# Two units earlier: the casts and copies of V in a fused window attention and MLP

## Chip, cores and metric

One core of a Trainium2 chip. The metric is the time on the device in microseconds (us) of one execution of the whole kernel; inputs and output lie in the chip's memory (HBM), and each time is a median over several runs.

The engines are named as the profile names them: PE is TensorE (matmuls; PEld its weight loads), ACT is ScalarE, DVE is VectorE, POOL is GpSimd, SP is SyncE, which here does nothing but issue DMAs. Each engine works through its own queue of instructions in the order in which the program was written, and waits where an instruction needs something that is not there.

## The reference

Causal attention within a window of 64 positions (8 batches, 8 heads, 576 positions, 64 per head), then a layer norm, an MLP with ReLU and a residual:

```python
def _attn_ref(q, k, v):
    scores = scale * np.matmul(q, k.transpose(0, 1, 3, 2))
    rel = pos[:, None] - pos[None, :]
    mask = (rel >= 0) & (rel < window)
    scores = np.where(mask, scores, -1000000000.0)
    ...
    attn = attn / (np.sum(attn, axis=-1, keepdims=True) + 1e-09)
    return np.matmul(attn, v).astype(np.float32)

def _moe_ref(x, g_ln, w_ch1, w_ch2):
    xn = (x - mu) / np.sqrt(var + 1e-06) * g_ln
    ch = np.maximum(xn @ w_ch1, 0.0) @ w_ch2
    return (x + ch).astype(np.float32)
```

`x` has 576 positions of 512 features in each batch; the hidden layer has 2048.

## The kernel before

**Blocks and stages.** The work is cut into nine groups of 512 positions. Groups 0 to 7 ("blocks") are the first 512 positions of each batch; group 8 collects the last 64 positions of all eight batches, in four "tails" of two batches each. The program runs one stage per group: stage `g` is the MLP of group `g`. The attention of the next block, `g+1`, is written in between, and so are the loads and the casts to fp16 of the block after it, `g+2`.

**Units and slots.** `mlp_units(g)` gives a list of small pieces of PE work. From stage 2 on they are 16 units `l1(hc)` (four matmuls of 128x512 each and one ReLU on ACT that writes `hrT`), then 14 units `product(n, t)` (eight matmuls of 128x256 each; some end in an addition on DVE, `post`). The loop at the end of the function writes unit `i`, then everything that was put in slot `i` with `at(i, f, ...)`, in the order in which it was put there. This alone sets the order of each engine's queue: nothing is moved afterwards. An instruction that is put at a later unit simply stands later in its engine's queue.

**One block's attention.** `s_mm(b, j)` (L326) makes the scores of a quarter of a block on PE, ACT takes the exponential into `pt` (`s_exp`, L347), DVE masks it (`s_mask`, L367), and `b_step(b, j)` (L383) multiplies by V. `b_step` then has DVE divide, take mean and variance (`mv`), and `r_step` has ACT make the reciprocal standard deviation from `mv` in two small instructions (L403, L404). `z_step` normalises on DVE (L414), and for quarters 0 to 2 a transposing DMA from SP (`x_step`, L461), for quarter 3 PE and ACT (`zt_step`, L450 and L453), turn it into `zT`, the MLP's input.

**V in two positions.** A window of 64 queries needs its own 64 keys and the 64 before them. `b_step` therefore reads V from two tiles: `vA`, the fp16 cast of the block's V, and `vB`, the same shifted by half a group of partitions. From block 3 on (`b >= NPE`) positions are interleaved in pairs, and `make_vB` copies `vA` to `vB` by four DMAs from POOL: for each half `j` (0 and 64) a copy of a whole run of 32 partitions, all four chunks `c` (L205, 130 KB), and a copy of the other 32 partitions for the first three chunks, shifted by one chunk (L206, 97.5 KB). `b_step(b, 0)` reads chunk 0 of `vB`, which the L206 copies don't write. `keep_v` (L132) then copies the last positions of V for the tails, two small DMAs more. All three are put in slots of stage `b - 2`; `b_step(b, 0)` stands at unit 4 of stage `b - 1`.

**The step around the change.** In stages 2 to 5 the casts for block `n = g + 2` all stand in the products of the stage, and on ACT: four of q and k (`cast_q`, L143, 128x1024), whose results SP transposes by DMA (`x_main`, L279 and L283), and four of V (`cast_v`, L143, 128x512, one for each chunk `c`). Between them ACT has `r_step` of the last quarter of block `g+1` (from `steps`, slot 19) and its `zt_step` copy (slot 23). Block 3 is prepared in stage 1, with its casts on POOL, but by the same `make_vB`. SP's queue goes from `x_main` straight on to the loads of q, k and V for the next block, and POOL's from `keep_v` to the stores of the stage's output (L469).

**The tails.** The table `TAILS[6]` puts the preparation of group 8 into stage 6: `load_tail`, `cast_tail` (part 0 is q and k, parts 1 and 2 are V into the tile `vt8`; the last argument says whether ACT or POOL casts), `x_tail` (the transposing DMA, L292), `x_prev` (a copy of the keys before the tail, on ACT for tails 1 to 3, L300), and the first scores. A row with `b_step` in slot `u` also puts its `r_step` in slot `u + 1` and its `z_step` in slot `u + 2`.

**PSUM buffers.** The results of `l1` and of the products share a pool of two buffers (`mm`) and another of two (`tp`); a matmul that starts a new result waits until the buffer that it was given has been read by ACT or DVE.

Of the kernel before, what the change touches and what calls it, by code (L numbers as in the profile page):

```python
# [18 lines left out]
def kernel(  # L19
# [182 lines left out]
    def make_vB(b):  # L202
        if b >= NPE:
            for j in range(0, 128, 64):
                nc.gpsimd.dma_start(out=vB[b][j + 32:j + 64, :], in_=vA[b][j:j + 32, :])  # L205
                nc.gpsimd.dma_start(out=vB[b][j:j + 32, 1:4], in_=vA[b][j + 32:j + 64, 0:3])  # L206
            return
        nc.gpsimd.dma_start(out=vB[b][64:128, :], in_=vA[b][0:64, :])
        nc.gpsimd.dma_start(out=vB[b][0:64, 1:4], in_=vA[b][64:128, 0:3])
# [231 lines left out]
    def pace(t):  # L441
        nc.gpsimd.tensor_copy(out=tok, in_=t)
# [302 lines left out]
    def tail_casts(i, act, *us):  # L745
        return tuple((u, cast_tail, i, part, act) for part, u in enumerate(us))
# [3 lines left out]
            *tail_casts(0, False, 7, 9, 9), (8, x_tail, 0), (8, x_prev, 0), (8, load_tail, 2, 0), (8, load_tail, 2, 1),  # L750
            *tail_casts(1, False, 10, 12, 12), (11, x_tail, 1), (12, load_tail, 3, 0), (12, load_tail, 3, 1),
            (18, x_prev, 1), (17, s_mm, 8, 0), (21, s_mask, 8, 0), *tail_casts(2, True, 19, 20, 20), (19, x_tail, 2), (20, x_prev, 2),
            *tail_casts(3, True, 22, 25, 25), (23, x_tail, 3), (25, x_prev, 3), (24, b_step, 8, 0),
            (24, s_mm, 8, 1), (26, s_mask, 8, 1)),
        7: ((1, b_step, 8, 1), (1, s_mm, 8, 2), (3, s_mask, 8, 2), (3, zt_step, 8, 0),
            (6, b_step, 8, 2), (6, s_mm, 8, 3), (8, s_mask, 8, 3), (7, zt_step, 8, 1),
# [2 lines left out]
    for g in range(NGRP):  # L759
# [3 lines left out]
        def at(i, f, *a):  # L763
            slots[min(i, len(slots) - 1)].append((f, a))
# [72 lines left out]
        if g == 1:  # L837
# [19 lines left out]
            for c in range(4):  # L857
                at(5 + c, cast_v, 2, c, c + 1)
            at(8, make_vB, 2)
            at(9, keep_k, 1)  # L860
            at(9, keep_v, 1)
# [38 lines left out]
        if 0 < g and b + 1 < B:  # L900
            n = b + 1
            e = 3 if g == 1 else 1
            at(e, load_qk, n, 0)
            at(e + 1, load_qk, n, 1)
            at(e + 4, load_v, n, 0, 4)
            if g == 1:
                at(10, alloc_qkT, n)
                for j, (x, half) in enumerate(((0, 0), (1, 0), (0, 1), (1, 1))):
                    u = (16, 19, 22, 25)[j]
                    at(u, lambda j=j: pace(rcps[(b, j)][:, 0:1]))  # L910
                    at(u, cast_q, n, x, half)
                at(20, x_main, n, 0)
                at(26, x_main, n, 1)
                at(19, alloc_v, n)
                at(19, alloc_vB, n)
                for u, c, j in ((21, 0, 0), (22, 1, 0), (25, 2, 1), (27, 3, 2)):
                    at(u, (lambda j=j: pace(zT[b][:, 0, 128 * j:128 * j + 1])) if c % 2 == 0 else
                       (lambda j=j: pace(rss[(b, j)])))
                    at(u, cast_v, n, c, c + 1)
                at(27, make_vB, n)  # L920
                at(27, keep_v, n)
            else:
                at(6, keep_k, b)
                at(3, alloc_qkT, n)
                for u, x, half in ((16, 0, 0), (16, 1, 0), (17, 0, 1), (19, 1, 1)):
                    at(u, cast_q, n, x, half, True)
                at(18, x_main, n, 0)
                at(21, x_main, n, 1)
                at(18, alloc_v, n)
                at(18, alloc_vB, n)  # L930
                for c in range(4):
                    at(21 + c, cast_v, n, c, c + 1, True)
                at(25, make_vB, n)
                at(25, keep_v, n)
        for i, u in enumerate(units):
            cur[0] += 1
            u()
# [34 lines left out]
```

## Time and profile before

| | us |
|---|---|
| median of 13 runs | 313.02 (310.42 to 317.29) |
| the profiled execution | 313.63 |
| its span, first to last instruction | 311.7 |
| PE busy in the span | 289.3 |
| ACT busy | 190.7 |
| DVE busy | 192.6 |
| POOL busy | 104.0 |

How to read the rows of a profile. In a timeline a row is: start in us from the span's start, duration, engine, line of the kernel, operation, tile written `<-` tiles read, shapes, and how many like instructions were merged; in square brackets, where the engine was idle before it, for how long and what ended the wait. The durations of neighbours on one engine overlap a little, because an engine starts on the next instruction before the last one has left it. A row of the waits is: who waited `<-` for whom: us in total, times, the longest. A DMA's row on an engine is only the time that the issue takes; how long the data take until they have landed is shown apart.

The page divides the span in 40 slices; PE's clock is granted in full in all but the last, and the mean granted clock is 0.996.

### The profile page before, as it was taken

Reading aid. Unit: us, or ns where it says so; the run is one execution under the profiler, and the core shown is the slowest. Engines: PE = TensorE matmul, PEld = TensorE weight load, DVE = VectorE, ACT = ScalarE, POOL = GpSimd, SP = SyncE. Lnnn points to the kernel's source line nnn. Section 1 sums busy time; section 2 is a strip of 40 time slices with the busy share of each in tenths; the row PEclk is TensorE's granted clock in tenths of the full one; section 3 lists DMA queues with packets and bytes.
Section 4 is the critical chain, followed back from the end, with each engine's and each line's share of the span. In section 5 each row is a group of like instructions: output and inputs, shape, how many; then the busy total and the mean of one; then the engine's idle time right before and its main releaser. Section 6 shows DMA issues by size and latency. Waiting matters only on the chain.

```text
span 311.7 us, 7942 instructions
## 1 busy us (share of the span) xinstructions
PE 289.3 (93%) x3259; PEld 186.8 (60%) x3259; DVE 192.6 (62%) x353; ACT 190.7 (61%) x372; POOL 104.0 (33%) x193
## 2 busy tenths in 40 slices
PE   5678999999998999799989996999999999999993
PEld 2446544865844578347845783479557844784582
DVE  0676337367854896289638952897389866742361
ACT  1688743676935875587558744885685967406500
POOL 3669765996674004300340043002363010000000
PEclk9999999999999999999999999999999999999998
DMA  7999999999959989997998999859998940003005
GB/s 178 257 381 331 316 279 291 270 304 260 201 85 296 214 100 201 287 212 93 219 284 207 99 215 281 199 77 187 264 146 155 158 152 2 2 0 135 2 0 135
DMA packets 115379, 58.23 MB, mean 187 GB/s; under 512 B 82048, under 2 KB 108160, under 8 KB 115344
## 3 DMA queue, kind: packets, MB, share of 16 engines
q1 hardware_dynamic: 110672, 45.50, 68.8%
q0 software_dynamic: 3712, 11.72, 11.9%
q10 hardware_dynamic: 960, 0.53, 0.6%
q8 instruction: 25, 0.41, 0.6%
q14 instruction: 10, 0.08, 0.1%
HBM read 36.70 MB, written 9.44 MB: 148 GB/s over the span
## 4 chain that ended last, share of the span: by engine, by line
PE 67%; DMA 15%; DVE 4%; SPq 4%; POOL 3%; ACT 3%; issue 2%; ACTq 0%; POOLq 0%; DVEq 0%
PE hps L509 27%; PE wX L587 12%; DMA vB<-vA 11%; PE wZ L587 6%; PE hph L546 5%; PE wY L587 4%; PE xps L383 4%; PE ch L560 3%; DMA w1s<-in_moe_w_ch_dram 2%; SPq L171 2%; PE sc L326 2%; DMA qk<-in_k_dram 2%; SPq L81 1%; ACT vA L143 1%; PE ztp L450 1%
## 5 line engine op out<-in xcount | busy, mean ns | idle before, releaser
L509 PE MATMUL hps<-zT,w1g 128*128 128x512 f16 x480 | 109.9, 379 | 0.7 <-ACT hrT L513 0.7
L513 ACT ACTIVATE hrT<-hps 128x512 f16<-128x512 f32 x120 | 71.3, 596 | 50.4 <-PE hps L509 49.2
L509 PEld LDWEIGHTS <-w1g 128*128 128x128 f16 x480 | 44.9, 98 | 50.4 <-issue 1.0
L587 PEld LDWEIGHTS <-sw 128*128 128x128 f16 x448 | 43.5, 98 | 5.0
L205 POOL DMA_DIRECT2D vB<-vA x10 | 5.1, 510 | 98.5 <-ACT vA L143 98.2
L587 PEld LDWEIGHTS <-hrT 128*128 128x128 f16 x336 | 32.4, 98 | 5.4
L367 DVE TENSOR_TENSOR pt<-pt,mask 128x1024 f16<-128x1024 f16 x28 | 20.8, 743 | 20.3 <-ACT pt L347 12.6
L347 ACT ACTIVATE pt<-sc 128x512 f16<-128x512 f32 x40 | 23.7, 594 | 9.1 <-PE sc L326 9.1
L469 POOL DMA_DIRECT2D out_dram<-osb x20 | 13.1, 658 | 47.6 <-DVE osb L605 43.5
L392 DVE BATCH_NORM_STATS2 stats<-xn 128x6 f32<-128x512 f32 x36 | 25.0, 694 | 1.2
L390 DVE TENSOR_TENSOR xn<-xps,rcp 128x512 f32<-128x512 f32 x36 | 24.9, 691 | 1.2
L546 PE MATMUL hph<-zT,w1g 128*128 128x256 f16 x192 | 23.7, 273 | 1.6 <-POOL w1g L235 1.6
L498 DVE TENSOR_TENSOR sw<-hrT 128x1024 f16<-128x1024 f16 x28 | 19.0, 677 | 9.7 <-ACT hrT L513 9.7
L383 PEld LDWEIGHTS <-pt 128*64 128x64 f16 x576 | 12.2, 110 | 20.4 <-issue 15.4
L414 DVE TENSOR_SCALAR z<-xn,mv,rs 128x512 f16<-128x512 f32 x32 | 17.8, 557 | 10.3 <-ACT rs L404 10.1
L387 DVE RECIPROCAL rcp<-xps 128x8 f32<-128x8 f32 x36 | 7.4, 204 | 23.1 <-PE xps L383 23.1
L383 PE MATMUL xps<-vB,pt 128*64 128x65 f16 x256 | 14.3, 197 | 7.7 <-DMA vB<-vA 6.2
L546 PEld LDWEIGHTS <-w1g 128*128 128x128 f16 x192 | 17.9, 98 | 4.6 <-POOL w1g L235 2.0
L353 ACT ACTIVATE pt<-sc 128x512 f16<-128x512 f32 x32 | 17.4, 595 | 5.0 <-PE sc L333 4.5
L605 DVE TENSOR_TENSOR osb<-wX,xn 128x512 f32<-128x512 f32 (+1 forms) x24 | 14.9, 620 | 8.8 <-PE wX L587 8.8
L522 PE MATMUL ch<-w2s,hrT 128*128 128x512 f16 x80 | 19.7, 379 | 0.0
L145 POOL CAST qk<-qk 128x1024 f16<-128x1024 f32 x16 | 16.5, 1040 | 9.1 <-DMA qk<-in_q_dram 6.3
(105 smaller groups left out, 438.1 us busy)
## 6 DMA issues: line engine op xcount, KB each, us to landing
qk<-in_q_dram SPq DMA_DIRECT2D x16, 512.0 KB, 5.9
qk<-in_k_dram SPq DMA_DIRECT2D x16, 512.0 KB, 7.7
w2s<-in_moe_w_ch_dram SPq DMA_DIRECT2D x12, 512.0 KB, 7.2
out_dram<-osb POOLq DMA_DIRECT2D x12, 512.0 KB, 7.9
v<-in_v_dram SPq DMA_DIRECT2D x40, 128.0 KB, 6.0
v<-in_v_dram SPq DMA_DIRECT2D x12, 256.0 KB, 6.4
w1s<-in_moe_w_ch_dram SPq DMA_DIRECT2D x4, 512.0 KB, 7.3
out_dram<-osb POOLq DMA_DIRECT2D x8, 256.0 KB, 6.0
```

Of the source, the lines that this page charges most:

```text
L347: nc.scalar.activation(out=pt[:, par].rearrange("k h w (p j) -> k (h w) p j", j=4), in_=sc[:, :].rearrange("k h w (j p) -> k (h w) p j", j=4),
L367: nc.vector.tensor_tensor(out=ptv, in0=ptv, in1=mb, op=ALU.mult)
L383: nc.tensor.matmul(out=xps[64 * r:64 * r + 64, h, :D + 1], lhsT=pt[:, par, hp, r, :], rhs=rhs, start=True, stop=True)
L390: nc.vector.tensor_tensor(out=xn, in0=xps[:, :, 0:D], in1=rcp_b, op=ALU.mult)
L392: nc.vector.bn_stats(out=stats, in_=xn.rearrange("p h d -> p (h d)"))
L414: nc.vector.tensor_scalar(out=z, in0=x, scalar1=mv[:, 0:1], scalar2=rss[(g, kb)][:, 0:1], op0=ALU.subtract, op1=ALU.mult)
L498: nc.vector.tensor_tensor(out=S[i], in0=a, in1=b, op=op)
L509: nc.tensor.matmul(out=hps, lhsT=w1g[:, kc, 128 * hc:128 * (hc + 1)], rhs=zT[g][:, kc, :], start=(kc == KCS[0]), stop=(kc == KCS[-1]),)
L513: nc.scalar.activation(out=hrT[:, hc, :], in_=hps, func=AF.Relu, bias=0.0, scale=1.0)
L522: nc.tensor.matmul(out=ch[kb], lhsT=hrT[:, hc, 128 * kb:128 * (kb + 1)], rhs=w2s[:, hc, :], start=(hc == 0), stop=(hc == NHC - 1),)
L546: nc.tensor.matmul(out=hps[:, e], lhsT=w1g[:, kc, 128 * hc:128 * (hc + 1)], rhs=zT[g][:, kc, 256 * half:256 * half + 256], start=(kc == KC ...
L587: nc.tensor.matmul(out=xyz[bank][t * two_banks][:, t], lhsT=lhsT, rhs=rhs, start=bool(first and (t == 0 or two_banks) and hc == 0), stop=( ...
```

## The change

It has three parts, all in the order of the program; no instruction is added or taken away.

1. In `make_vB` the two copies of whole runs are issued first, then the two shifted ones. This holds for blocks 3 to 7.
2. In stages 2 to 5 the fourth cast of q and k goes from slot 19 to 18, V's casts from slots 21 to 24 to slots 18, 20, 20 and 21, the transposes from 18 and 21 to 17 and 19, `make_vB` and `keep_v` from 25 to 22, and the two allocations with their memsets from 18 to 16.
3. In stage 6 the V casts of the last tail go from slot 25 to 27, behind `r_step` of group 8's first quarter (slot 25), and `x_prev` of that tail goes from 25 to 23.

```diff
@@ make_vB
             for j in range(0, 128, 64):
                 nc.gpsimd.dma_start(out=vB[b][j + 32:j + 64, :], in_=vA[b][j:j + 32, :])
+            for j in range(0, 128, 64):
                 nc.gpsimd.dma_start(out=vB[b][j:j + 32, 1:4], in_=vA[b][j + 32:j + 64, 0:3])
@@ TAILS[6]
-            *tail_casts(3, True, 22, 25, 25), (23, x_tail, 3), (25, x_prev, 3), (24, b_step, 8, 0),
+            *tail_casts(3, True, 22, 27, 27), (23, x_tail, 3), (23, x_prev, 3), (24, b_step, 8, 0),
@@ stages 2 to 5
-                for u, x, half in ((16, 0, 0), (16, 1, 0), (17, 0, 1), (19, 1, 1)):
+                at(16, alloc_v, n)
+                at(16, alloc_vB, n)
+                for u, x, half in ((16, 0, 0), (16, 1, 0), (17, 0, 1), (18, 1, 1)):
                     at(u, cast_q, n, x, half, True)
-                at(18, x_main, n, 0)
-                at(21, x_main, n, 1)
-                at(18, alloc_v, n)
-                at(18, alloc_vB, n)
+                at(17, x_main, n, 0)
+                at(19, x_main, n, 1)
                 for c in range(4):
-                    at(21 + c, cast_v, n, c, c + 1, True)
-                at(25, make_vB, n)
-                at(25, keep_v, n)
+                    at((18, 20, 20, 21)[c], cast_v, n, c, c + 1, True)
+                at(22, make_vB, n)
+                at(22, keep_v, n)
```

## The prediction

> **What bounds the kernel now.** I read the page first, then the waits of the whole core, then the timelines of TensorE (PE), ScalarE (ACT) and GpSimd (POOL) around each wait that remained. "Stage g" is the MLP pass over block g; the attention of block g+1 and the loads and casts of block g+2 run inside it.
>
> The page's span and its row of busy times:
>
> ```profile
> span 311.7 us, 7942 instructions
> PE 289.3 (93%) x3259; PEld 186.8 (60%) x3259; DVE 192.6 (62%) x353; ACT 190.7 (61%) x372; POOL 104.0 (33%) x193
> ```
>
> PE is idle for 22.4 us in all. Before 27 us (start-up) and after 306 us (the last stores) the change touches nothing. In between, PE runs matmul to matmul except where two rows of the waits say otherwise (who waits, for whom; us in total, times, longest):
>
> ```profile
> PE xps L383 <- DMA vB<-vA: 6.2, 4, 2.4
> ...
> PE hps L509 <- ACT hrT L513: 0.7, 1, 0.7
> ```
>
> PE's timeline shows where they lie. Besides a first one of 1.36 us at 99.65 and one of 0.81 us at 161.89 (the text uses both), they are:
>
> ```profile
> 131.22 0.19 PE L383 MATMUL xps<-vB,pt 128*64 128x65 f16 x1 [1.72 <-DMA vB<-vA]
> 194.11 0.19 PE L383 MATMUL xps<-vB,pt 128*64 128x65 f16 x1 [2.37 <-DMA vB<-vA]
> 251.73 1.02 PE L509 MATMUL hps<-zT,w1g 128*128 128x512 f16 x4 [0.75 <-ACT hrT L513]
> ```
>
> So the first `b_step` of blocks 3, 4, 5 and 6 (in stages 2 to 5) waits 1.36 + 1.72 + 0.81 + 2.37 = 6.26 us for shifted V copies. Between those four starts the windows give PE 29.86 us of work in 31.57, 30.67 and 32.22 us: PE is the bound and the wait is the whole rest. Stage 6, where nothing waits for a copy, shows no gap.
>
> Why the copies are late: ACT's timeline in stage 2, at its end, and then POOL's.
>
> ```profile
> 112.46 2.92 ACT L143 CAST qk<-qk 128x1024 f16<-128x1024 f32 x3
> 116.81 0.29 ACT L403 ACTIVATE rs<-mv,epst 128x1 f32<-128x1 f32 x1 [1.42 <-DVE mv L394]
> 117.13 0.20 ACT L404 ACTIVATE rs<-rs 128x1 f32<-128x1 f32 x1
> 117.24 1.03 ACT L143 CAST qk<-qk 128x1024 f16<-128x1024 f32 x1
> 118.18 1.14 ACT L143 CAST vA<-v 128x512 f16<-128x512 f32 x2
> 119.50 0.59 ACT L453 COPY zT<-ztp 128x512 f16<-128x512 f16 x1 [0.19 <-PE ztp L450]
> 119.99 1.14 ACT L143 CAST vA<-v 128x512 f16<-128x512 f32 x2
> ```
>
> ```profile
> 121.42 0.51 POOL L205 DMA_DIRECT2D vB<-vA  x1 [24.45 <-ACT vA L143]
> 121.92 0.50 POOL L206 DMA_DIRECT2D vB<-vA  x1
> 122.41 0.49 POOL L205 DMA_DIRECT2D vB<-vA  x1
> ```
>
> ACT stands idle for 1.42 us in front of `r_step`, later for `ztp`, with four V casts still to do. POOL, idle for 24.45 us, starts the copies 0.29 us after the last cast. The first `b_step` reads vB at c = 0, which only the two L205 ("whole") copies write; the second is issued third, at 122.41. The chain of waits has it 8.67 us in flight; PE starts 0.14 us after it lands.
>
> **The change, part by part.** It removes and adds no instruction. In the two builds the order of PE, VectorE (DVE) and SP is the same; POOL's changes only by the swap of copies; ACT's changes in stages 2 to 5 and at the tail.
>
> *V casts (stages 2 to 5).* New ACT order: three casts, the fourth q/k cast, V cast 0, `r_step` (two instructions), V casts 1 to 3, zT copy. In stage 2: a q/k cast has a pitch of 0.95 us (2.92 less its 0.07 overlap, over 3), so the fourth starts at 115.31 and V cast 0 at 116.26 (17.24 to 18.18 gives 0.94). A V cast has a pitch of 0.52 (1.14 for two of 0.62), so ACT is free at 116.78; mv is ready at 116.77, and `r_step` stays at 116.81. Its pair takes 0.43, then the last three V casts run 117.24 to 118.90. Before, the last ended at 121.13: 2.23 us earlier. In stages 3 to 5 ACT idles 1.34 to 1.35 us there, 0.08 less, so `r_step` slips by 0.1 us at most. What waits for it is `z_step` on DVE, which in stage 3 starts at 149.36, 0.53 after rs ends at 148.83, behind other DVE work: that cover hides the slip. If it were gone the slip would reach PE's `ztp` (150.66, after z ends at 149.90), with 0.76 us more to spare.
>
> *Copies.* Whole copy 1 now goes out second: 118.90 + 0.29 + 0.51 = 119.70 in place of 122.41, 2.71 us earlier. How long it flies then is the unknown. In this trace (DMA view, one issue at a time) the two 130 KB copies take 5.5 and 7.5 us for block 3, 7.5 and 8.7 for block 4, 7.4 and 7.7 for 5, 8.6 and 9.3 for 6, and for block 7, beside which SP loads only the small tails, 3.1 and 5.6. With the slowest, 9.3 us, it lands at 129.00 and PE could go at 129.14. PE wants it at 131.22 - 1.72 = 129.50. The same sum for block 5: issue 154.01 - 2.71 = 151.30, ready 160.74, wanted 161.08; for block 6: 181.97, 191.41, 191.74. So even the slowest flight closes all three waits, by 0.3 us; the nearest row (block 3's first copy, issued 0.35 us after SP's first 512 KB load, as the moved one is 0.14 us before it) has 5.5 us and 4 us to spare. I take 1.72 + 0.81 + 2.37 = 4.90 us, all of it.
>
> What is late next there: the mask of `pt` on DVE (128.07 + 0.69 = 128.76), 0.74 us ahead of 129.50, so no wait takes the place of this one.
>
> *The swap alone (block 3, whose casts in stage 1 stay on POOL).* Whole copy 1 moves from third to second, 0.5 us earlier. The part copy that had the second place landed 0.71 us before it (98.80 against 99.51). But the whole copy is a third larger (130 against 97.5 KB). Ends: 0, if its own size sets its landing, and 1.2, place and issue together. I take 0.4 of the 1.36 us.
>
> *SP and POOL queues.* `x_main` is moved in program order past nothing on SP: its four transposes start at 114.37, 115.72, 117.10 and 118.49, a pitch of 1.35 to 1.39 that SP's own issue sets, and the earlier fourth cast (116.33 against 118.27) lets the last one go at about 118.45. So the next block's loads (119.84) start as before. On POOL the two vt copies and the two out stores behind `make_vB` follow; the first store waits for DVE's osb (123.00 + 0.69), so it gains 0.7 us at most, behind vB anyway. The memsets of `alloc_v` and `alloc_vB` keep their places. V itself has landed: in stage 2 the last V load lands at 112.24, the first cast now runs at 116.26.
>
> The copies now go out at 119.2 to 121.2 us, where DVE is at fp16 and fp32 TENSOR_TENSORs, and not from 121.4 on, where it is half free. One row has such company: the store issued at 73.83, wholly inside DVE's fp16 TENSOR_TENSORs (73.40 to 74.68), took 0.57 us, against 0.54 to 0.55 for POOL's other stores near it. So I charge nothing. A rule speaks against that: the Trainium skill, page "SBUF — State Buffer", section "SBUF: two separate sides", says that GpSimd cannot write a DMA's descriptors while VectorE runs an operation that takes the port pair they share, and the next section has such a DMA grow from about 620 to 3100 ns. By the rule one such delay, an estimate of 2.5 us, would eat 2.5 of the 2.71 us; the three waits would shrink by 0.2 us each and the execution would stand at 312.0.
>
> *Tail (stage 6).* The ACT rows that move:
>
> ```profile
> 246.88 1.09 ACT L353 ACTIVATE pt<-sc 128x512 f16<-128x512 f32 x2
> 247.99 1.26 ACT L143 CAST vt<-tv 64x512 f16<-64x512 f32 x2
> 249.16 0.61 ACT L300 COPY tqkT<-kprev 128x512 f16<-128x512 f16 x1
> 249.68 0.29 ACT L403 ACTIVATE rs<-mv,epst 128x1 f32<-128x1 f32 x1
> ```
>
> New order: L300, the two exps, `r_step`, the two vt casts. mv is there at 247.19 + 0.18 = 247.37. L300 runs at 246.88 (it waits for old transposes of block 7, landed by 216), the exps at 247.40, rs at 248.51 and not 249.68: 1.17 us earlier. The exps end 0.5 us later and the mask behind them comes after z on DVE anyway. On DVE, z (250.24), mask and the wZ add (251.30) move to 249.07, 249.53 and 250.13, done at 250.81. In the changed build the second hps tile of stage 7 waits for DVE instead of ACT: it takes the buffer that the wZ add frees, no longer the one that the first hrT frees. PE wants it at 250.98 by the trace, so 0.75 us go, or none if DVE is late by as much. I take 0.65. The vt casts (249.0 to 250.2) end before ACT's first hrT (251.08) can start; without that gap they would cost up to 1.2 us there.
>
> *Sum:* 4.90 + 0.40 + 0.65 = 5.95 us. The profiled execution took 313.63 us, its span 311.7, so 1.9 lie around it: 313.63 - 5.95 = 307.7. That execution is 0.6 above the median of 313.02, and some of this may be longer waits than the median run has. I halve it: **307.4 us**.
>
> **The rivals.**
>
> 1. *The copies land little earlier* (chance 0.07). They now fly beside the last K transposes, and if flight grows by what issue gains, only the swap stays: 0.5 us in each of four stages and 0.65 at the tail, 313.0 - 2.65 = 310.4. For it: flight varies from 3.1 to 9.3 us with company. Against: the longest flights are those issued 2.6 us behind the loads.
> 2. *No change: the DMA queues are the bound* (0.07). Stages show a DMA share of 0.95 to 1.04, and a shorter PE stage would wait for loads or transposes instead, all but the tail's 0.65: 312.4. Against: the share falls to 0.11 at 112.4 to 114.4, so DMAs wait for PE's side there, and stage 5 to 6 ran in 29.79 us.
> 3. *Slower: the K transposes* (0.06). The copies, moved into them, hold up the last qkT transpose, started 118.49, which takes 3.3 us. The next stage's first scores (125.50) need it. From a flight of 7.0 us on it costs PE the excess, in four stages. The V waits are gone all the same, so it decides from a flight of 8.5 us (4 x 1.5 = 6.0). If company adds to it what it adds to a copy (9.3 against 3.1, 6.2 us), it flies 9.5: 4 x 2.5 = 10 us lost, 313.0 + 10.0 - 5.95 = 317.1. Against: today these transposes already overlap the first loads and still take 3.1 to 3.3 us.
>
> **How the numbers follow.** The forecast has 0.80. Its own bounds: all waits gone, 313.63 - 7.0 less 0.6 = 306.0, to one missed stage, about 309.5. Runs of one kernel scatter over 310.4 to 317.3, so the median moves by itself; low is 305.4. High is 310.9, which takes in rival 1. A measurement tells no change from a gain only beyond about 0.5%, 1.6 us. Faster than 311.4: the forecast, rival 1, a little of rival 2: 0.87. Same: 0.07. Slower: 0.06.
>
> **What would show it.** The last V cast of a stage ends ahead of the zT copy; POOL's two L205 rows stand together; the row "PE xps L383 <- DMA vB<-vA" falls from 6.2 us to about 1, all of it at the first place; the row of hps and hrT is gone; stages take 29.9 us. It is wrong if flights of vB grow past 9.6 us, if L326 begins to wait for qkT, or if SP's transposes start later against PE than now.

## The result, and the profile after

| | before | after |
|---|---|---|
| median, us | 313.05 (48 runs, 310.4 to 318.6) | 308.53 (11 runs, 307.6 to 311.1) |
| the profiled execution, us | 313.63 | 307.56 |
| its span, us | 311.7 | 305.7 |
| PE busy in the span, us | 289.3 | 289.1 |

The ratio of after to before is 0.9887, with a 95% interval of 0.986 to 0.9913: of 313.0 us, 3.5 us are gone (2.7 to 4.4). The two medians stand 4.5 us apart; the ratio leaves out runs that were over 1.5% above the fastest of their kernel. The change is faster, and the predicted 307.4 us lies 1.1 us under the median. The profiled execution of the changed kernel is the fastest of its eleven.

The page of the changed kernel, its span and its row of busy times:

```profile
span 305.7 us, 7942 instructions
PE 289.1 (95%) x3259; PEld 186.7 (61%) x3259; DVE 192.1 (63%) x353; ACT 190.4 (62%) x372; POOL 104.3 (34%) x193
```

The busy times are those of before to within 0.5 us. What went is idle time of PE: 22.4 us before, 305.7 - 289.1 = 16.6 now. Lines behind L204 stand one lower in the changed kernel, so L383 is now L384 and L509 is L510. The waits of the changed kernel (who waits `<-` for whom: total, times, longest):

```profile
PE xps L384 <- DMA vB<-vA: 1.3, 1, 1.3
```

Of 6.2 us in four waits, one wait of 1.3 us is left. PE's timeline says which. Behind 77 us, where the first `b_step` of block 2 starts, these are its only two gaps of over 0.12 us ahead of the last stores:

```profile
99.39 0.19 PE L384 MATMUL xps<-vB,pt 128*64 128x65 f16 x1 [1.29 <-DMA vB<-vA]
...
245.81 1.02 PE L510 MATMUL hps<-zT,w1g 128*128 128x512 f16 x4 [0.18 <-DVE osb L606]
```

The first is block 3's, in stage 2. Blocks 4, 5 and 6 start at 129.18, 158.97 and 188.76 us: three stages of 29.79 us each, where there were 31.57, 30.67 and 32.22. The second is the tail's: it waits for DVE and no longer for ACT, and for 0.18 us and not 0.75.

ACT's timeline at the end of stage 2, and then POOL's:

```profile
112.21 3.87 ACT L143 CAST qk<-qk 128x1024 f16<-128x1024 f32 x4
115.98 0.62 ACT L143 CAST vA<-v 128x512 f16<-128x512 f32 x1
116.55 0.30 ACT L404 ACTIVATE rs<-mv,epst 128x1 f32<-128x1 f32 x1
116.88 0.20 ACT L405 ACTIVATE rs<-rs 128x1 f32<-128x1 f32 x1
116.98 1.65 ACT L143 CAST vA<-v 128x512 f16<-128x512 f32 x3
119.25 0.59 ACT L454 COPY zT<-ztp 128x512 f16<-128x512 f16 x1 [0.62 <-PE ztp L451]
```

```profile
118.92 1.00 POOL L205 DMA_DIRECT2D vB<-vA  x2 [22.13 <-ACT vA L143]
119.92 0.99 POOL L207 DMA_DIRECT2D vB<-vA  x2
```

The gap of 1.42 us in front of `r_step` is filled with a q/k cast and a V cast, and the last V cast ends ahead of the zT copy, at 118.63. The two whole copies (L205) stand together. All of stage 2 lies 0.26 us earlier than before (99.39 against 99.65), and with these 0.26 the predicted times (`r_step` 116.81, the last cast's end 118.90, the first copy 119.19) are those of the rows, to 0.01 us.

The DMA view, over the same work of block 4, before (first fence) and after (second). A row is: what, queue, kind and count, KB each, median us from issue to landing.

```profile
vB<-vA POOLq DMA_DIRECT2D x2, 130.0 KB, 8.1
```

```profile
vB<-vA POOLq DMA_DIRECT2D x2, 130.0 KB, 5.1
```

The whole copies are issued earlier *and* fly for 3 us less. The experiments are mostly about this shorter flight, which the prediction left as "the unknown".

### The profile page after: what moved, and what is told of

Same layout as the page of the kernel before. It is cut to its first block, busy times and chain, and to the rows that moved or that the text cites. A ratio compares the mean times of both kernels' runs of the same rounds, so it can differ in the third digit from the quotient of the medians.

```text
span 305.7 us, 7942 instructions
## 1 busy us (share of the span) xinstructions
PE 289.1 (95%) x3259; PEld 186.7 (61%) x3259; DVE 192.1 (63%) x353; ACT 190.4 (62%) x372; POOL 104.3 (34%) x193
## 4 chain that ended last, share of the span: by engine, by line
PE 72%; DMA 8%; DVE 7%; SPq 5%; ACT 2%; POOL 2%; issue 2%; POOLq 0%; DVEq 0%; ACTq 0%
PE hps L510 31%; PE wX L588 14%; PE wZ L588 7%; PE hph L547 5%; PE wY L588 4%; PE xps L384 4%; PE ch L561 3%; DMA vB<-vA 3%; DMA w1s<-in_moe_w_ch_dram 2%; PE sc L327 2%; SPq L171 2%; DMA qk<-in_k_dram 2%; DMA tqk<-in_k_dram 1%; SPq L81 1%; DVE stats L393 1%
## 5 line engine op out<-in xcount | busy, mean ns | idle before, releaser
L510 PE MATMUL hps<-zT,w1g 128*128 128x512 f16 x480 | 109.9, 379 | 0.2 <-DVE osb L606 0.2
L510 PEld LDWEIGHTS <-w1g 128*128 128x128 f16 x480 | 44.9, 98 | 49.8 <-issue 0.5
L205 POOL DMA_DIRECT2D vB<-vA x10 | 5.1, 516 | 84.2 <-ACT vA L143 83.9
L384 PEld LDWEIGHTS <-pt 128*64 128x64 f16 x576 | 12.2, 110 | 15.4 <-issue 10.3
L454 ACT COPY zT<-ztp 128x512 f16<-128x512 f16 x21 | 12.3, 585 | 9.7 <-PE ztp L451 9.6
```

The source lines that it names most:

```text
L384: nc.tensor.matmul(out=xps[64 * r:64 * r + 64, h, :D + 1], lhsT=pt[:, par, hp, r, :], rhs=rhs, start=True, stop=True)
L510: nc.tensor.matmul(out=hps, lhsT=w1g[:, kc, 128 * hc:128 * (hc + 1)], rhs=zT[g][:, kc, :], start=(kc == KCS[0]), stop=(kc == KCS[-1]),)
```

## The experiments

Each kernel ran on the same chip as the kernel before, several rounds of each; ratios are to that kernel.

**1 to 3: each part alone.** First the swap in `make_vB`:

```diff
             for j in range(0, 128, 64):
                 nc.gpsimd.dma_start(out=vB[b][j + 32:j + 64, :], in_=vA[b][j:j + 32, :])
+            for j in range(0, 128, 64):
                 nc.gpsimd.dma_start(out=vB[b][j:j + 32, 1:4], in_=vA[b][j + 32:j + 64, 0:3])
```

> The kernel before with the two whole copies of make_vB issued first, and nothing else. Theory (the earlier V casts close the waits; the swap is worth what it showed at block 3, 1.36 to 1.29 us): all four waits for vB stay, at about 6 us in all, the time falls by 0.1 to 0.5 us. Rival (the swap does it, since the first b_step reads the whole copies alone): the waits fall by 0.5 us and more each, 2 to 5 us in all.

Measured: 0.9942 (0.9909 to 0.9976), some 1.8 us, more than was expected. The waits of its profiled execution:

```profile
PE xps L384 <- DMA vB<-vA: 3.9, 3, 1.7
```

They are 1.70 us at 77.78 (block 2, which `make_vB` copies in another branch), 0.80 at 100.30 (block 3) and 1.36 at 191.11 (block 6); blocks 4 and 5 wait for nothing. The expectation had all four waits of before stay; two are gone, and those of stages 2 to 5 come to 2.16 us, so the rival fits better. A likely reason, not shown by a run of its own: with the casts where they were, all of blocks 3 to 6 wait for the second whole copy, and each gets it up to 0.5 us earlier, 2.0 us in all.

Then the casts alone (the lines of stages 2 to 5 of the diff, without the swap and the tail):

> The kernel before with the casts, transposes and copies of stages 2 to 5 at their new slots; the copies in the old order, the tail as before. Theory: the waits for vB in stages 3 to 5 are gone (4.90 us), the first one of 1.36 us and the 0.75 us at the tail stay; about 4.9 us off the profiled span. Rival (swap and casts are needed together): waits of 0.5 us or so stay in stages 3 to 5, half of the gain or less.

Measured: 0.9905 (0.9877 to 0.9933), some 3.0 us: most of the change's effect. Its waits and the two places they have:

```profile
PE xps L383 <- DMA vB<-vA: 4.1, 2, 2.1
```

```profile
77.94 0.19 PE L383 MATMUL xps<-vB,pt 128*64 128x65 f16 x1 [2.08 <-DMA vB<-vA]
...
101.71 0.19 PE L383 MATMUL xps<-vB,pt 128*64 128x65 f16 x1 [2.05 <-DMA vB<-vA]
```

Stages 3 to 5 are free of them. What is left stands at blocks 2 and 3, whose casts this part doesn't touch, and is larger than in the profile of before, where block 2 waited for no copy and block 3 for 1.36 us. These two waits differ from execution to execution.

Then the tail alone (the row of `TAILS[6]`):

> The kernel before with the new slots of the last tail's V casts and x_prev alone. Theory: the wait of the second hps tile of stage 7 falls from 0.75 to about 0.2 us, everything else stays: 0.55 us off. Rival (the tail's gain came from stages that end earlier, not from the order on ScalarE): the wait stays at 0.75 us and the time does not change.

Measured: 1.0006 (0.9973 to 1.0039): nothing that can be told from no change. The profile shows the mechanism nevertheless:

```profile
250.70 1.02 PE L509 MATMUL hps<-zT,w1g 128*128 128x512 f16 x4 [0.42 <-DVE osb L605]
```

The wait falls from 0.75 to 0.42 us and changes its releaser from ACT to DVE. This kernel has casts and copies in their old order, and its waits in stages 3 to 5 were 0, 1.03 and 1.52 us: 2.55 where the profile of before had 4.90. In turn its blocks 2 and 3 waited for copies for 1.43 and 1.70 us, where before had 0 and 1.36. All waits for vB together differ less, 5.68 against 6.26 us.

**4: half the way.** `make_vB` only three slots earlier, all V casts behind `r_step` as before:

```diff
                 for c in range(4):
-                    at(21 + c, cast_v, n, c, c + 1, True)
-                at(25, make_vB, n)
-                at(25, keep_v, n)
+                    at((21, 22, 22, 22)[c], cast_v, n, c, c + 1, True)
+                at(22, make_vB, n)
+                at(22, keep_v, n)
```

> The kernel before with V's four casts in stages 2 to 5 put ahead of the zT copy (slots 21, 22, 22, 22) and make_vB and keep_v in slot 22; the fourth q/k cast stays behind r_step, copies in the old order. The last V cast ends about 0.8 us earlier, not 2.2. Theory 1 (only the issue counts, the flight of a copy stays 7.7 to 9.3 us): waits in stages 3 to 5 of 0.9, 0 and 1.6 us, 2.5 in place of 4.9. Theory 2 (a copy issued closer to the first loads also flies shorter, as in the changed kernel, where flights fell to 4.0 to 5.5 us, some 1.3 us for each us of issue): waits of 0, 0 and about 0.5 us.

Measured: 0.9979 (0.9943 to 1.0016), waits of 0, 0.21 and 0.86 us in stages 3 to 5. The waits lie between the two accounts and settle nothing. The second whole copy, issued 1.8 us behind SP's first load instead of 2.6, still flew 6.1, 8.0 and 8.6 us.

**5: the change once more,** unchanged, to see how its waits vary.

> The changed kernel once more, beside the runs that follow and with a profile of another execution. Theory: no wait for vB in stages 3 to 5 in this execution either (at most 0.2 us); the tail's second hps tile waits 0.2 to 0.4 us; what differs from the first profile lies ahead of 105 us, at the copies of blocks 2 and 3 (up to 2 us each), which the change leaves with their old casts. Rival (the first profile was a lucky one): waits of 0.5 us and more in stages 3 to 5. Time 308 to 309 us.

Measured: 0.9885 (0.9843 to 0.9928), the ratio of the first time. Again no wait for vB in stages 3 to 5, and 0.95 us in stage 2. The tail is worse than expected:

```profile
245.44 1.02 PE L510 MATMUL hps<-zT,w1g 128*128 128x512 f16 x4 [0.94 <-DVE osb L606]
```

0.94 us is more than the 0.75 of the old order.

**6: do the copies fly long because of SP's loads?** The kernel before, with every cast and copy in its old place, but block `n+1`'s first load (and so all behind it in SP's queue) held until POOL has issued the copies. A memset of one element on POOL writes into the tile that the load will fill; the load waits for it.

```diff
+    def hold(b):
+        held[b] = p_in.tile([128, 1024], FP32, tag="qk32_0", name=f"qk32_0_{b}_0")
+        nc.gpsimd.memset(held[b][0:1, 0:1], 0.0)
...
                 at(25, make_vB, n)
+                if n + 1 < B:
+                    at(25, hold, n + 1)
```

> The kernel before, with casts, copies and tail as they were; one memset of a single element on POOL, placed behind make_vB, of the buffer that SP's next load of q writes, so that SP's loads for blocks 5 to 7 start about 3 us later, behind the issue of the copies. The copies go out as late as before. Theory 2 (company sets the flight): the second whole copy flies 4 to 5.6 us in place of 7.7 to 9.3, and the waits of stages 3 to 5 are gone or under 0.3 us each; the first wait and the tail stay. Theory 1 (the issue alone counts): the waits stay at what other executions of this order show, 2.5 to 4.9 us in all for stages 3 to 5.

Measured: 0.9877 (0.982 to 0.9934). POOL's timeline, then SP's (lines are seven lower here):

```profile
121.32 0.51 POOL L212 DMA_DIRECT2D vB<-vA  x1 [24.57 <-ACT vA L150]
121.83 0.50 POOL L213 DMA_DIRECT2D vB<-vA  x1
122.32 0.50 POOL L212 DMA_DIRECT2D vB<-vA  x1
122.81 0.50 POOL L213 DMA_DIRECT2D vB<-vA  x1
123.34 0.09 POOL L80 MEMSET qk<- 1x1 f32 x1
```

```profile
123.46 0.39 SPq L98 DMA_DIRECT2D qk<-in_q_dram  x1
```

The copies go out as late as ever (121.32 and 122.32 us, against 121.42 and 122.41), the loads 3.6 us later than before. And the DMA view:

```profile
vB<-vA POOLq DMA_DIRECT2D x2, 130.0 KB, 2.5
...
qkT<-qk SPq DMA_TRANSPOSE x4, 3.3
```

Issued at the same time, the copies fly 2.5 us and not 8.1, less than either account had expected, and no wait for vB is left in stages 3 to 5. So copies cast as late as ever are in time once none of SP's 512 KB loads is ahead of them: with the copies issued when they were, it is these loads that made the flight long. The flights of the second whole copy of blocks 4, 5 and 6, by its place against SP's first load, from eight traces:

| kernel | issued, against the first load | flights, us |
|---|---|---|
| before | 2.6 to 2.7 us behind | 8.7, 7.7, 9.3 |
| the tail alone | 2.6 to 2.7 behind | 6.9, 8.0, 8.5 |
| the swap alone | 2.1 to 2.2 behind | 7.0, 7.4, 8.8 |
| half the way | 1.8 behind | 6.1, 8.0, 8.6 |
| the casts alone | 0.1 to 0.4 behind | 7.2, 5.5, 5.6 |
| the change | 0.1 ahead | 5.1, 5.5, 4.2 |
| the change once more | 0.1 ahead | 5.0, 5.7, 5.3 |
| loads held | 1.1 to 1.3 ahead | 2.6, 2.8, 2.7 |

The place does not settle a single flight: block 4's copy flew 6.9 us at 2.6 us behind (the tail alone) and 7.2 at 0.3 behind (the casts alone).

The Trainium skill, page "DMA: Bandwidth & Descriptors", section "Queues, rings and completion order", says that each DMA engine serves the queue rows it has work for in turn, packet by packet. With two rows in work that would, as an estimate, double a copy's time; the copies just ahead of the loads do fly about twice 2.5 us, those 2 us and more behind the first load mostly take three times the 2.5 us, which a doubling does not give. Whether the packets of the two queues are of one size was not looked at.

**7: the slower rival, provoked.** The changed kernel with all four V casts and `make_vB` ahead of the q/k casts, so that all copies meet the K transposes:

```diff
-                for u, x, half in ((16, 0, 0), (16, 1, 0), (17, 0, 1), (18, 1, 1)):
+                for u, x, half in ((18, 0, 0), (18, 1, 0), (20, 0, 1), (20, 1, 1)):
...
-                at(17, x_main, n, 0)
-                at(19, x_main, n, 1)
+                at(19, x_main, n, 0)
+                at(21, x_main, n, 1)
...
-                    at((18, 20, 20, 21)[c], cast_v, n, c, c + 1, True)
-                at(22, make_vB, n)
-                at(22, keep_v, n)
+                    at((16, 16, 17, 17)[c], cast_v, n, c, c + 1, True)
+                at(18, make_vB, n)
+                at(18, keep_v, n)
```

> The changed kernel with ScalarE's order in stages 2 to 5 turned over: the four V casts first (slots 16, 16, 17, 17), copies in slot 18, then the q and k casts (18, 18, 20, 20) and their transposes (slots 19 and 21). The copies go out about 4 us earlier still, the last transpose about 2 us later. Theory (the waits are already gone and the transposes have some 3 us to spare): the same time as the changed kernel, within 0.5%. Rival (the last transpose of k is the next bound, and the copies now fly in the midst of the transposes): a wait of the scores L327 for qkT of 0.5 to 2 us in each of four stages, 2 to 8 us slower than the changed kernel.

Measured: 0.993 (0.9896 to 0.9964); its median of 310.56 us (310.05 without one run of 315.81) lies above the changed kernel's on the same chip, 308.50. The two intervals overlap, so the time makes it likely, but does not show, that this order is slower. The DMA view of stage 2's end, and PE's timeline at the start of stage 4:

```profile
vB<-vA POOLq DMA_DIRECT2D x2, 130.0 KB, 3.0
...
qkT<-qk SPq DMA_TRANSPOSE x4, 7.0
```

```profile
156.09 0.32 PE L327 MATMUL sc<-qkT,qkT 64*64 64x64 f16 x16 [0.43 <-DMA qkT<-qk]
...
156.85 0.32 PE L327 MATMUL sc<-qkT,qkT 64*64 64x64 f16 x16 [0.44 <-DMA qkT<-qk]
```

The copies land fast (the second whole one in 3.7 to 4.1 us), and the transposes fly 7.0 us and not 3.3. SP's issue of the last three of four takes 1.97 to 3.41 us where it took 1.29, so they also start later. The same holds at stage 3's end, where the first three fly 7.3, 8.1 and 6.7 us, and there it is too late: at the start of stage 4 the scores wait for `qkT`, 0.87 us in two waits. That is one stage of four, and about half of the 1.5 to 2.1 us between the medians; block 2's wait (0.82 us) and the tail's (0.54) vary in any kernel, and the rest wasn't traced further.

**8 to 11: the wait that the change leaves.** Block 3's copies are cast on POOL in stage 1. Two of its four V casts go to ACT (with them go the two small POOL instructions, `pace`, that stood in front of them) and the copies two slots forward:

```diff
-                for u, c, j in ((21, 0, 0), (22, 1, 0), (25, 2, 1), (27, 3, 2)):
+                for u, c, j in ((21, 0, 0), (22, 1, 0)):
...
-                at(27, make_vB, n)
-                at(27, keep_v, n)
+                for c in (2, 3):
+                    at(24, cast_v, n, c, c + 1, True)
+                at(25, make_vB, n)
+                at(25, keep_v, n)
```

> The changed kernel with the last two V casts of block 3 (stage 1) on ScalarE in slot 24 and make_vB and keep_v in slot 25. Theory (a copy that is issued ahead of the next loads flies 4 to 5.5 us): the copies of block 3 go out about 1.4 us earlier, ahead of SP's first load, and the wait of stage 2, 1.3 to 2 us, is gone; 1 to 2 us less than the changed kernel, 307 us. Rival (block 3's copies fly 7.5 us and more for other reasons): the wait stays at 0.5 us or more.

Measured: 0.983 (0.9803 to 0.9858), median 307.07 us. The DMA view at block 3, in the changed kernel and then here:

```profile
vB<-vA POOLq DMA_DIRECT2D x2, 130.0 KB, 6.7
```

```profile
vB<-vA POOLq DMA_DIRECT2D x2, 130.0 KB, 3.4
```

Issued 1.36 and 0.84 us ahead of SP's first load instead of 0.36 and 0.88 behind it, the whole copies fly 2.5 and 4.3 us, and block 3's wait is gone. The interval lies just under that of the changed kernel's first series (0.986 to 0.9913) and overlaps that of its second (0.9843 to 0.9928). One wait for vB is left, block 2's:

```profile
77.54 0.19 PE L384 MATMUL xps<-vB,pt 128*64 128x65 f16 x1 [1.65 <-DMA vB<-vA]
```

The same for block 2 as well, two of its V casts on ACT:

```diff
-                at(5 + c, cast_v, 2, c, c + 1)
+                at((5, 6, 8, 8)[c], cast_v, 2, c, c + 1, c > 1)
```

> As block3_act, and the last two V casts of block 2 on ScalarE as well (slot 8 of stage 1), so that its copies go out about 1 us earlier. Theory: the wait before block 2's first b_step, which came to 1.4 to 2.1 us in four of six profiled executions, falls by 1 us; median 0.5 to 1 us below block3_act, about 306.3 us. Rival (PE waits there for its own buffer or for mask and scores as well): no change against block3_act.

Measured: 0.9848 (0.9805 to 0.9891), which overlaps the run without it: inconclusive. Its profiled execution, at 311.01 us the longest of its six, is not read.

Then the cure of experiment 6 for block 2: on top of the casts for block 3, block 3's V load (1 MB, in SP's queue beside block 2's copies) waits for a one-element memset that stands behind these copies on POOL. Beside it the kernel with block 3's casts on ACT once more, without the hold.

```diff
+    def hold_v(b):
+        v32[b] = p_in.tile([128, 4, H, D], FP32, tag="v32", name=f"v32_{b}", bufs=1)
+        nc.gpsimd.memset(v32[b][0:1, 0, 0, 0:1], 0.0)
...
-            at(e + 4, load_v, n, 0, 4)
+            if g == 1:
+                at(8, hold_v, n)
+            at(e + 4 + (g == 1), load_v, n, 0, 4)
```

> block3_act with the same trick for block 2: a memset of one element on POOL behind block 2's make_vB, of the buffer that the V loads of block 3 write, so that these start about 1.4 us later, behind the copies' issue. Theory (company sets the flight): block 2's copy lands 0.5 to 1.5 us earlier and the wait before its first b_step (1.65 us in block3_act's profile) shrinks by as much, about 0.5 to 1 us less than block3_again. Rival (that copy's company is the q and k loads of block 3, already under way): no change against block3_again.

> block3_act once more, beside block3_hold. The ratio to the kernel before is 0.980 to 0.986 again; no wait for vB from stage 2 on.

Measured: 0.9768 (0.9733 to 0.9803) with the hold, median 306.47 us; 0.9807 (0.976 to 0.9854) without, median 307.60. The intervals overlap, so the hold's own share is not shown. Nor do the profiles show it. PE's timeline at block 2 with the hold, and without:

```profile
76.83 0.19 PE L388 MATMUL xps<-vB,pt 128*64 128x65 f16 x1 [0.85 <-DMA vB<-vA]
```

```profile
76.70 0.19 PE L384 MATMUL xps<-vB,pt 128*64 128x65 f16 x1 [1.27 <-DVE tw L487]
```

Without the hold block 2 waited for no copy at all in this execution, but for DVE. With the hold the V load went out 1.16 us behind block 2's first copy instead of 0.27 ahead of it. That copy (260 KB) flew 5.3 us, in the midst of the 4.4 to 6.5 us of the eleven other profiles read. So the rival, that other loads already under way are this copy's company, stands.

The kernel with the hold is the fastest of the study, and its interval lies clear of the changed kernel's (0.986 to 0.9913).

## Why the prediction was right, and where its sizes were off

*V casts and copies.* The issue times came true to 0.01 us, and all three waits of stages 3 to 5 went, as forecast, each stage taking 29.79 us. By the prediction's sum the 2.7 us of earlier issue alone would have ended the waits. The runs show a second thing beside it: the copies now stand 0.1 us ahead of SP's first load, and fly 4.2 to 5.5 us where they flew 7.7 to 9.3. The prediction bounded the flight by 9.3 us and named 5.5 as the nearest row; these flights show that it was the right row. Experiment 6 shows that the shorter flight is enough without an earlier issue; no run has the earlier issue without the shorter flight.

*The size of that term, 4.90 us.* This is the term that was mis-sized. It is what these waits cost in the one execution that was profiled. Another execution of the same order of casts and copies (the tail alone) had 2.55 us. The gain was 3.5 us (2.7 to 4.4) by the ratio, 4.5 by the medians, and not 5.6, and the prediction's allowance for a typical run, 0.3 us, was too small. In the profiled executions themselves the sum holds: the span fell by 6.0 us against 5.95. That close an agreement is partly luck: the profiled execution of before took 0.6 us more than its kernel's median and that of the changed kernel 1.0 less. The 6.0 us part as follows: 0.26 us up to block 3's start, 5.09 in stages 3 to 5, 0.6 behind them.

*The swap, 0.40 us at block 3.* In the profile it gave 0.07 (1.36 to 1.29). The second whole copy went out 0.5 us earlier and flew 7.9 us and not 7.5, which is near the end of 0 in the bounds; whether its size or its company held it, no run separates. Alone, with the old casts, the swap is worth 0.6% (0.2 to 0.9), and its profile has 1.36 us of waits in stages 3 to 5, where the moved casts make it needless. The parts therefore need not add: 0.58% and 0.95% would make 1.5, and the whole has 1.1; the intervals are too wide to tell.

*The tail, 0.65 us of 0.75.* The profile gave 0.57, and the wait's new owner is the one that was named, DVE's addition. But it is not steady. In five profiles of the old order the wait was 0.74 or 0.75; in seven of the new (all but the run of 311.01 us) it was 0.18, 0.42, 0.94, 0.54, 0.40 and twice nothing. The mean is 0.35, a gain of about 0.4 us, under what the time can show (experiment 3).

*What is late next.* Nothing: no mask and no score waits in stages 3 to 5. The last K transpose flies 5.1 and 4.6 us in the two stages for which the changed kernel's trace has it, where it flew 3.1 to 3.3. So the slower rival's mechanism is at work, inside the 7.0 us that were free; experiment 7 takes it out of them.

*The rivals.* That the copies land little earlier (310.4 us) fell with the flights of the table. That the DMA queues are the bound (312.4) fell with stages of 29.79 us. The slower one needed 8.5 us of flight and got 5.1.

*The port rule.* The four copies issued at 118.92 to 120.91 us, beside DVE's TENSOR_TENSORs, took 0.50 us each, as they did elsewhere. The delay that the Trainium skill ("SBUF — State Buffer", "SBUF: two separate sides") describes for an operation that takes the shared port pair is not seen, and charging nothing was right. No run shows whether these operations take that pair.

*Open.* Why block 2's large copy flies 4.4 us in one execution and 6.5 in another, why block 3's wait with its old casts runs from 0.80 to 2.05 us, and how much of the scatter between runs comes from this: with block 3's wait gone, the same kernel still ran over 305.9 to 308.3 us in one series and 306.6 to 310.2 in the other, one run of 311.5 apart. Whether the hold for block 2 or chance made the fastest kernel 1.1 us faster than its twin.

## What to carry to other kernels

A small copy that an engine will wait for belongs ahead of the bulk loads, not merely earlier: its flight here was some 2.5, 5 or 8 us by its place against SP's 512 KB loads, and holding the loads back was worth as much as casting sooner, within the noise. Idle time of an engine in front of a dependency (ACT's 1.42 us) is where work from behind can go for nothing. Waits on DMAs differ between executions, so what a wait costs is better taken from several profiles than from the one at hand.

## What the runs showed of the hardware that was not expected

DMA transposes and copies between on-chip tiles disturb each other strongly: with block 4's copies in the queues beside them (experiment 7), transposes took 7.0 us from issue to landing instead of 3.3, and the issue of one up to 3.41 us instead of 1.29; the copies of 97.5 KB took 6.0 us there and 2.8 where SP's loads were held. The same copy of 130 KB took 2.3 to 3.0 us with SP's loads held behind it and 9.3 at most behind loads. And a wait that comes from ACT was the same to 0.01 us in five executions (0.74 to 0.75), while its successor on DVE ran from nothing to 0.94.
